# Scale and bias on VectorE in the last pair of heads, with four smaller moves of work in a fused attention, MoE and ELU kernel

## The chip, the core and the metric

The kernel runs on one core of one Trainium2 chip. The core has TensorE (matrix products, with a row of its own in the profile for the loading of weights), VectorE, ScalarE, GpSimd and SyncE, which work in parallel, each in the order of its own instruction list, and wait for each other through semaphores. The metric is the device time of one execution in microseconds (us), the median of several runs.

## What is computed

Three stages follow each other. In the reference, cut to what matters:

```python
# attention: 2 batches x 8 heads, 768 tokens, 64 channels; 6 random projections give each token a bucket
q_bucket = sum((q @ proj > 0) * 2**bit);  k_bucket = sum((k @ proj > 0) * 2**bit)
scores = where(q_bucket == k_bucket, q @ k.T / 8, -1e9)
attn = softmax(scores);  x = attn @ v                     # x: 1536 tokens x 512
# mixture of 8 experts, one for each token
e = argmax(x @ w_gate);  gate = softmax(x @ w_gate)[e];  eom = sigmoid(x @ w_output_gate)[e]
x = gate * eom * (relu(x @ w1[e]) @ w2[e])
# dense layer
h = x @ w_in;  out = where(h > 0, h, exp(min(h, 0)) - 1) @ w_out
```

## The kernel before

Attention goes through 96 query tiles of 128 tokens (8 pairs of heads, 12 tiles a pair), numbered n = 0 to 95. A hand-written software pipeline issues, in pass n of one loop, stages of several tiles; every engine then works off its own list in that order. For one tile the stages are:

- stage_S, TensorE: four matmuls give the 128 x 768 scores in PSUM (tile `s`, two buffers).
- stage_M: VectorE takes the negated row maximum `nm` of the scores (L369); GpSimd turns it into a scale `sc` (L370, zero or 2^64) and a bias `bi` (L371), one number for each of the 128 rows.
- stage_E, ScalarE: the exponential `p` of the scores with that bias and scale, and the row sums (L378).
- stage_T: six TensorE transposes of `p` into PSUM tiles `t` (three buffers, shared with some other small tiles); ScalarE copies each rounded to `pthi` (L402), VectorE makes the remainder `ptlo` (L405 for the second half of a tile, run one pass later, and L407 for the first half). A buffer `t` is free when `ptlo` is made.
- stage_V, TensorE: four matmuls a pass with the values `vst`; after three passes the output `o` is copied out (stage_O), in the last two pairs with an addition on VectorE (L447).

So in a pass VectorE does, in this order: `nm` of the tile before, the late `ptlo`, whatever was queued for this pass in the list `early`, the first `ptlo`. Other work is attached to passes by `at(n, f)`, which runs f at the end of pass n. The heads of the next pair are prepared on the way: `load_pair` loads them on SyncE's queue, `prep_T` splits them into `qhi`/`qlo` and `khi`/`klo` (one buffer each), and `restack` copies these by DMA into the operands `qa`, `qb`, `ka`, `kb`.

The gate of a batch (`gate`) is a list of small steps on 128 x 48 or 128 x 24 elements: logits, maximum, one-hot `oh`, softmax weight, rank of each token in its expert by matmuls into PSUM (`rank`), that rank times `oh` (`g_rk`), the row `rown`, its integer `idx`, and counts of tokens (`count`, `lt`, `count_lt`, `count_all`). The first batch's gate is spread over the passes 63 to 87 by `gate_first`; a scatter by row numbers `idx` follows from pass 85 on GpSimd. The second batch's gate runs in two halves after the last tile (gates 2 and 3). Expert 0's inputs from these halves are then gathered by matmuls with selection matrices `sel`: `part_rows` makes `row0` from `g_rk` and `oh` (L917), `part_sel` compares `row0` with `ranks` (L927), `part_rest` makes the remainders `xlo` (L937), and TensorE adds up `xacc` (L944). After that come the experts' products (from about 255 us) and the dense layer (to the end).

Of the kernel before, what the change touches and what calls it, by code (L numbers as in the profile page):

```python
# [13 lines left out]
ALU = mybir.AluOpType  # L14
AX = mybir.AxisListType
# [4 lines left out]
UNIT = float(2.0 ** 64)  # L20
# [5 lines left out]
def kernel(  # L26
# [19 lines left out]
    nc = tc.nc  # L46
# [14 lines left out]
    CAP = 224  # L61
# [6 lines left out]
    XC = DM + 16  # L68
# [7 lines left out]
    w8 = const.tile([128, E], F32, name="w8")  # L76
    nc.gpsimd.iota(w8, pattern=[[-1, E]], base=E, channel_multiplier=0, allow_small_or_imprecise_dtypes=True)
    ranks = const.tile([128, CAP], BF16, name="ranks")
    nc.gpsimd.iota(ranks, pattern=[[1, CAP]], base=0, channel_multiplier=0, allow_small_or_imprecise_dtypes=True)
    tok = const.tile([128, B, NC], I32, name="tok")  # L80
    nc.gpsimd.iota(tok, pattern=[[S, B], [1, NC]], base=0, channel_multiplier=NC)
    ones_b = const.tile([128, 128], BF16, name="ones_b")
# [3 lines left out]
    with nc.allow_low_precision("multiples of 256 below 2 ** 14 of at most 6 bits, exact"):  # L86
# [3 lines left out]
        tri_b, ones_b, pattern=[[1, 128]], compare_op=ALU.is_gt, fill=0.0, base=0, channel_multiplier=-1  # L90
# [60 lines left out]
    zt0 = ap1.tile([128, XC], F32, name="zt0")  # L151
# [210 lines left out]
    def stage_M(n):  # L362
        hd, c = tile_of(n)
        if c == 0:
            sums[hd] = ap2.tile([128, NC], F32, tag="sums", name="sums", bufs=3)
        nm = ap2.tile([128, 1], F32, tag="nm", name="nm", bufs=3)
        bi = ap2.tile([128, 1], F32, tag="bi", name="bi", bufs=3)
        sc = ap2.tile([128, 1], F32, tag="sc", name="sc", bufs=3)
        nc.vector.tensor_reduce(nm, sps[n][:, :, 0:HC], AX.XY, ALU.max, negate=True)  # L369
        nc.gpsimd.tensor_scalar(sc, nm, 0.25, UNIT, ALU.is_lt, ALU.mult)  # L370
        nc.gpsimd.tensor_tensor(bi, sc, nm, ALU.mult)  # L371
        soft[n] = (bi, sc)

    def stage_E(n):
# [161 lines left out]
    box = {}  # L536
# [3 lines left out]
    def gate(gi, n=HALF):  # L540
# [18 lines left out]
        eq, d, ed, oz, rk = (t3(x) for x in ("eq", "d", "ed", "oz", "rk"))  # L559
        lt = t3("lt", BF16)  # L560
        oh = ohs[:, gis].rearrange("p g c e -> p (g c) e")
        rw_n = rown[:, gis].rearrange("p g c -> p (g c)")
# [5 lines left out]
        V = nc.vector  # L568
        P = V if b == B - 1 else nc.gpsimd

        def rank():
            if n == HALF:
                ps = small_psum(sh, gi == NG - 2)
            else:
                ps = sps[max(sps)][:, 0, HC:HC + n * E].rearrange("p (c e) -> p c e", e=E)
            nc.tensor.matmul(ps, ones_b, eb_b[:, 0:n], start=True, stop=False)
            nc.tensor.matmul(ps, tri_b, oh, start=False, stop=False)
            for i in range(1, n):
                nc.tensor.matmul(ps[:, i:], ones_b, oh[:, :n - i], start=False, stop=(gi == 0 and i == n - 1))
            if gi:  # L580
                for i in range(n):
                    nc.tensor.matmul(ps[:, i], ones_b, cnt[:, gi, 0], start=False, stop=(i == n - 1))

            def mine():
                V.tensor_tensor(rk, ps, oh, ALU.mult)

            if n == HALF:
                mine()
            else:
                early.append(mine)  # L590

# [15 lines left out]
        def count_all():  # L607
# [16 lines left out]
            rank,  # L624
            weight,
            lambda: V.reciprocal(xg[:, :, DM:DM + 1], gg[:, :, None]),
            lambda: V.tensor_reduce(rw_n, rk, AX.X, ALU.add),
            lambda: V.tensor_copy(idx, rw_n),
        ]
        after = [  # L630
            count,
            lambda: V.tensor_tensor(lt, bc(fm), w8b, ALU.is_gt),
            count_lt,
            count_all,
        ]
# [7 lines left out]
            scat.append(i)  # L643
            spacer()

        box[gi] = (oh, rk, eq)
        return main, after, [lambda c=c: scatter(c) for c in range(n)]

    def spacer():
# [10 lines left out]
    def both(fs):  # L660
        for f in fs:
            f()

    load_pair(1, "q")
    def keep_warm(n, end=False):
        ps = (ps_t if end else ps_o).tile([128, HC], F32, tag="t" if end else "o", name="warm")
        for i in range(n):
# [25 lines left out]
    qhi_evac, qlo_evac = prep_T(0, "q", 1)  # L693
    qhi_evac()
    bit_weights()
    load_pair(0, "v")

    def place(nm, p0, t):
        nc.sync.dma_start(opnd[0, nm][p0:p0 + 64, HC:].bitcast(F32), t[0:64, HC:].bitcast(F32))
# [4 lines left out]
    def second_half():  # L704
        qlo_evac()
        place("qa", 64, qlo)
        for nm in "qk":
            prep_Zm(0, 1, nm)
        restack(0, "q", (1,))
        load_pair(1, "k")  # L710
        load_pair(1, "v")
# [10 lines left out]
    NQ = NH * NC  # L722
# [5 lines left out]
    def at(n, f, *a):  # L728
        todo.setdefault(n, []).append((f, a))
# [3 lines left out]
    def gate_first():  # L733
        main, after, scs = gate(0, NC)
        for n, fs in (
            (63, main[:4]), (64, main[5:6]), (67, main[4:5]), (73, main[6:10]), (75, main[10:11] + main[12:13] + after[:3]),
            (78, main[15:]), (79, main[11:12]), (81, main[13:14]), (82, main[14:15]), (87, after[3:]),
        ):
            for f in fs:
                at(n, f)  # L740
        for n, f in zip((85, 87, 88, 90, 91, 93), scs):
            at(n, f)
# [24 lines left out]
    for hh in range(2):  # L767
        at(10 + 2 * hh, joining_rows, rw, hh)
        at(14 + 4 * hh, joining_rows, rw_end, hh)
    for j in range(3):  # L770
        at(13 + 3 * j, nc.gpsimd.memset, zt0[:, j * XC // 3:(j + 1) * XC // 3], 0.0)
    for hh in range(2):
        at(12 + 3 * hh, load_gates, hh, False)
        at(61 + 3 * hh, load_gates, hh, True)
# [138 lines left out]
    parts = {}  # L913

    def part_rows(gi):
        oh, rk, _ = box[gi]
        nc.vector.scalar_tensor_tensor(parts[gi][0], rk[:, :, 0], -1.0, oh[:, :, 0], ALU.add, ALU.add)  # L917

    def part_tiles(gi):
        row0 = gate_p.tile([128, HALF], F32, tag="row0", name="row0", bufs=2)  # L920
# [582 lines left out]
```

## Time and profile before

| | |
|---|---|
| median of 3 runs | 704.16 us (703.58 to 704.34) |
| profiled execution, its own time | 704.39 us |
| its span, first to last instruction | 702.3 us |
| attention tiles (first to last `nm`) | 10.1 to 234.6 us |
| last pair (`nm` of tile 84 to `nm` of tile 95) | 209.25 to 234.56 us |
| granted TensorE clock, mean | 0.997 of full speed |

The profile covers one execution. Times in its rows are counted from the first instruction; 2.1 us of the execution's time lie outside the span. An entry in square brackets is the idle time of the engine before the instruction and what ended it.

### The profile page before, as it was taken

How to read it: one execution, taken by the hardware profiler on the slowest of the kernel's cores; microseconds unless marked ns; L12 is line 12 of the kernel's file. 1: busy time of each engine (PE TensorE's matmuls, PEld its weight loads, DVE VectorE, ACT ScalarE, POOL GpSimd, SP SyncE). 2: the span in 40 equal slices, each digit the busy share in tenths (PEclk: the TensorE clock that was granted, in tenths of full speed). 3: DMA queues.
4: the chain of work that ended last, by engine and by line, in shares of the span. 5: the costliest groups of instructions: out<-in, count | busy, mean ns of one | idle time of the engine just before them, and what ended most of it. 6: DMA issues, size and time to landing. Idle time of an engine off the chain costs nothing.

```text
span 702.3 us, 12093 instructions
## 1 busy us (share of the span) xinstructions
PE 688.6 (98%) x4120; PEld 616.4 (88%) x4121; DVE 553.1 (79%) x1026; ACT 427.8 (61%) x854; POOL 214.6 (31%) x503
## 2 busy tenths in 40 slices
PE   8999999999999999999999999999999999999996
PEld 5799999999999989999999998888888888888885
DVE  6999999999999897888888898877788447934433
ACT  5998998999888767666766664444543224422221
POOL 5676556555566640221235410000000000002012
PEclk9999999999999999999999999999999999999998
DMA  8747658667572259777788984222122000001011
GB/s 194 195 115 210 173 161 203 181 174 203 148 201 79 77 184 327 237 244 251 229 211 229 264 218 113 93 88 91 61 90 91 0 1 0 1 1 60 7 53 64
DMA packets 47476, 96.92 MB, mean 138 GB/s; under 512 B 11752, under 2 KB 23848, under 8 KB 47408
## 3 DMA queue, kind: packets, MB, share of 16 engines
q1 hardware_dynamic: 44944, 89.67, 45.2%
q0 software_dynamic: 2304, 6.40, 2.4%
q8 instruction: 35, 0.57, 0.3%
q14 instruction: 33, 0.27, 0.1%
q10 hardware_dynamic: 160, 0.00, 0.0%
HBM read 63.68 MB, written 10.72 MB: 106 GB/s over the span
## 4 chain that ended last, share of the span: by engine, by line
PE 52%; issue 34%; DMA 6%; DVE 5%; ACT 2%; POOL 1%; SPq 0%; DVEq 0%; POOLq 0%; ACTq 0%
PE hps L1186 12%; PE s L351 8%; PE yps L1199 8%; PE o L421 8%; PE t L400 7%; DMA out_dram<-part,tidt 5%; PE yps L1201 3%; PE sp L501 2%; DVE nm L369 2%; PE zps L280 1%; PE xTp L1168 1%; DVE ptlo L407 1%; DMA qb<-qhi 1%; DMA tidt<-tid_d 1%; PE xacc L944 1%
## 5 line engine op out<-in xcount | busy, mean ns | idle before, releaser
L378 ACT ACTIVATE p<-s,bi,sc 128x768 f32<-128x768 f32 x96 | 95.8, 998 | 4.7 <-POOL bi L371 4.3
L886 DVE TENSOR_TENSOR wl<-wraw,wh 128x1024 fp32r<-128x1024 f32 (+1 forms) x65 | 77.2, 1190 | 21.8 <-ACT wh L882 19.6
L1344 POOL DMA_INDIRECT out_dram<-part,tidt x12 | 11.5, 959 | 265.4 <-DVE part L1341 264.2
L369 DVE TENSOR_REDUCE nm<-s 128x1 f32<-128x768 f32 x96 | 90.6, 944 | 2.0 <-POOL vst L330 1.1
L1306 ACT ACTIVATE ee<-gps 128x512 f32<-128x512 f32 x48 | 28.7, 597 | 100.1 <-PE gps L1296 100.1
L402 ACT ACTIVATE pthi<-t 128x384 fp32r<-128x384 f32 x192 | 84.0, 493 | 7.6 <-PE t L400 6.3
L1199 PE MATMUL yps<-h,wh 128*128 128x448 f32 x256 | 84.5, 380 | 0.0
L400 PE MATMUL t<-ident,p 128*128 128x128 f32 x576 | 80.3, 273 | 2.0 <-DVE ptlo L405 1.1
L1296 PE MATMUL gps<-x2l,vh 128*128 128x512 f32 x192 | 75.9, 395 | 0.0
L1326 PE MATMUL a<-vh,gl 128*128 128x512 f32 x192 | 75.8, 395 | 0.0
L1296 PE MATMUL gps<-x2h,vl 128*128 128x512 f32 x192 | 75.7, 394 | 0.0
L1296 PE MATMUL gps<-x2h,vh 128*128 128x512 f32 x192 | 75.7, 394 | 0.0
L1326 PE MATMUL a<-vh,gh 128*128 128x512 f32 x192 | 75.5, 393 | 0.0
L1326 PE MATMUL a<-vl,gh 128*128 128x512 f32 x192 | 75.5, 393 | 0.0
L351 PE MATMUL s<-ka,qa 128*128 128x384 f32 x192 | 73.3, 383 | 1.8 <-DMA qa<-qlo 1.2
L400 PEld LDWEIGHTS t<-ident,p 128*128 128x128 f32 x576 | 68.1, 140 | 7.8 <-PE t L400 1.5
L1307 DVE TENSOR_SCALAR ee<-ee 128x512 f32<-128x512 f32 x48 | 20.4, 426 | 68.0 <-ACT ee L1306 67.9
L1309 ACT ACTIVATE gh<-ee 128x512 fp32r<-128x512 f32 x48 | 30.4, 633 | 69.0 <-DVE ee L1308 69.0
L421 PE MATMUL o<-pthi,vst 128*128 128x384 f32 x192 | 66.9, 348 | 0.3
L882 ACT ACTIVATE wh<-wraw 128x1024 fp32r<-128x1024 f32 x63 | 66.2, 1052 | 0.0
L351 PE MATMUL s<-kb,qb 82*128 82x384 f32 x192 | 65.2, 340 | 0.0
L421 PE MATMUL o<-ptlo,vst 128*128 128x384 f32 x192 | 64.9, 338 | 0.0
(238 smaller groups left out, 1783.9 us busy)
## 6 DMA issues: line engine op xcount, KB each, us to landing
wraw<-in_moe_w_t_dram SPq DMA_DIRECT2D x64, 512.0 KB
w<-in_moe_w_in_dram SPq DMA_DIRECT2D x16, 512.0 KB
w<-in_moe_w_out_dram SPq DMA_DIRECT2D x16, 512.0 KB
ka<-khi SPq DMA_DIRECT2D x30, 192.0 KB
xs_d<-zt SPq DMA_DIRECT2D x8, 528.0 KB
xs<-xs_d SPq DMA_DIRECT2D x7, 462.0 KB
raw_v<-in_v_dram SPq DMA_DIRECT2D x8, 384.0 KB
kb<-klo SPq DMA_DIRECT2D x15, 192.0 KB
```

The lines of the kernel that those rows point to most:

```text
L351: nc.tensor.matmul(ps[:, j, 0:HC], opnd[st, "q" + x][0:n1, cb], opnd[st, "k" + x][0:n1, j * HC:(j + 1) * HC], start=(x == "a"), stop=(x == ...
L369: nc.vector.tensor_reduce(nm, sps[n][:, :, 0:HC], AX.XY, ALU.max, negate=True)
L378: nc.scalar.activation(p.rearrange("p (a b) -> p a b", a=2), sps.pop(n)[:, :, 0:HC], AF.Exp, bias=bi, scale=sc, accum_out=sums[hd][:, c:c ...
L400: nc.tensor.transpose(ps[:, a, :], p[:, kt * 128:(kt + 1) * 128], ident)
L402: nc.scalar.activation(ho, ps, AF.Copy)
L421: nc.tensor.matmul(ops[m], vst[hd][:, kt, :], t[:, kt, :], start=(kt == 0 and x == 0), stop=(kt == NC - 1 and x == 1))
L882: eng_hi.activation(hi, r, AF.Copy)
L886: fs = [lambda c=slice(j, j + h): eng.tensor_tensor(lo[:, c], r[:, c], hi[:, c], ALU.subtract) for j in range(0, PW, h)]
L1186: nc.tensor.matmul(ps, w[:, dc, fs], x[:, dc], start=(i == 0), stop=(i == len(terms) - 1))
L1199: nc.tensor.matmul(ps, wh[:, f], h[:, :, f], start=(f == 0), stop=last)
L1296: nc.tensor.matmul(ps, w[:, dc], x[:, dc, th * TC:(th + 1) * TC], start=(dc == 0 and i == 0), stop=(dc == KD - 1 and i == 2),)
L1326: nc.tensor.matmul(ps, x[:, cs], w, start=(fb in first_fb and i == 0), stop=(fb in last_fb and i == 2))
```

## The change

Five edits:

1. In the last pair (passes that handle tiles 84 to 95) `sc` and `bi` are made on VectorE instead of GpSimd.
2. In the first batch's gate the counts `count`, `lt` and `count_lt` move from pass 75 to passes 86 and 87, `count_all` from 87 to 90, and `rown` and `idx` from pass 78 to 82.
3. For gates 2 and 3 `row0` is made straight from the rank sums in PSUM, `(ps + 1) * oh`, with `ranks` counted from 1 instead of 0; the product `g_rk` moves behind it, in front of `rown`.
4. On SyncE's queue the values of pair 0 are loaded where the transposed queries of pair 1 were, and those queries behind the copy of `qlo`.
5. The zero tile `zt0` is cleared in six pieces of 88 columns instead of three of 176.

```diff
-    nc.gpsimd.iota(ranks, pattern=[[1, CAP]], base=0, ...)
+    nc.gpsimd.iota(ranks, pattern=[[1, CAP]], base=1, ...)
...
         nc.vector.tensor_reduce(nm, sps[n][:, :, 0:HC], AX.XY, ALU.max, negate=True)
-        nc.gpsimd.tensor_scalar(sc, nm, 0.25, UNIT, ALU.is_lt, ALU.mult)
-        nc.gpsimd.tensor_tensor(bi, sc, nm, ALU.mult)
+        eng = nc.vector if n >= NQ - 12 else nc.gpsimd
+        eng.tensor_scalar(sc, nm, 0.25, UNIT, ALU.is_lt, ALU.mult)
+        eng.tensor_tensor(bi, sc, nm, ALU.mult)
...
             if n == HALF:
-                mine()
+                box[gi] = (oh, ps)
+                late.append(mine)
...
-            lambda: V.tensor_reduce(rw_n, rk, AX.X, ALU.add),
+            lambda: (both(late), V.tensor_reduce(rw_n, rk, AX.X, ALU.add)),
...
-    load_pair(1, "q")
+    load_pair(0, "v")
...
     bit_weights()
-    load_pair(0, "v")
...
         place("qa", 64, qlo)
+        load_pair(1, "q")
...
-            (63, main[:4]), (64, main[5:6]), (67, main[4:5]), (73, main[6:10]), (75, main[10:11] + main[12:13] + after[:3]),
-            (78, main[15:]), (79, main[11:12]), (81, main[13:14]), (82, main[14:15]), (87, after[3:]),
+            (63, main[:4]), (64, main[5:6]), (67, main[4:5]), (73, main[6:10]), (75, main[10:11] + main[12:13]),
+            (79, main[11:12]), (81, main[13:14]), (82, main[14:]), (86, after[:1]), (87, after[1:3]), (90, after[3:]),
...
-    for j in range(3):
-        at(13 + 3 * j, nc.gpsimd.memset, zt0[:, j * XC // 3:(j + 1) * XC // 3], 0.0)
+    for j in range(6):
+        at(11 + 3 * j // 2, nc.gpsimd.memset, zt0[:, j * XC // 6:(j + 1) * XC // 6], 0.0)
...
-        nc.vector.scalar_tensor_tensor(parts[gi][0], rk[:, :, 0], -1.0, oh[:, :, 0], ALU.add, ALU.add)
+        nc.vector.scalar_tensor_tensor(parts[gi][0], ps[:, :, 0], 1.0, oh[:, :, 0], ALU.add, ALU.mult)
```

Lines of the changed kernel stand one to four further down than those of the kernel before (`ptlo` L405 and L407 are L406 and L408 there). On SyncE's queue, the first loads of the program, before:

```order
L135 DMA raw_q<-in_q_dram 128x3x64 x4
L130 DMA raw_q<-in_q_t_dram 128x768
L303 DMA ka_134<-khi 64x768 x2
L303 DMA kb_135<-klo 64x768
L126 DMA raw_v<-in_v_dram 128x2x384
L699 DMA qa_128<-qhi 64x384
L699 DMA qb_129<-qhi 64x384
L699 DMA qa_128<-qlo 64x384
L303 DMA qa_132<-qhi 64x768
L303 DMA qa_132<-qlo 64x768
L303 DMA qb_133<-qhi 64x768
```

The same place with the change:

```order
L135 DMA raw_q<-in_q_dram 128x3x64 x4
L126 DMA raw_v<-in_v_dram 128x2x384
L303 DMA ka_134<-khi 64x768 x2
L303 DMA kb_135<-klo 64x768
L701 DMA qa_128<-qhi 64x384
L701 DMA qb_129<-qhi 64x384
L701 DMA qa_128<-qlo 64x384
L130 DMA raw_q<-in_q_t_dram 128x768
L303 DMA qa_132<-qhi 64x768
L303 DMA qa_132<-qlo 64x768
L303 DMA qb_133<-qhi 64x768
```

The values have moved three transfers forward, and pair 1's queries (`in_q_t_dram`) six, to just ahead of the three copies that restack head 1 of pair 0.

On VectorE, the passes around tile 86 (where `nm` of a tile, the two `ptlo`, the reciprocal of a row sum and the addition of an output follow each other), before:

```order
L369 TENSOR_REDUCE nm<-s 128x1
L405 TENSOR_TENSOR ptlo<-t,pthi 128x3x128
L407 TENSOR_TENSOR ptlo<-t,pthi 128x3x128
L468 RECIPROCAL ri<-sm 128x3
L369 TENSOR_REDUCE nm<-s 128x1
L405 TENSOR_TENSOR ptlo<-t,pthi 128x3x128
L447 TENSOR_TENSOR osb<-o,osb 64x384
L407 TENSOR_TENSOR ptlo<-t,pthi 128x3x128
```

The same place with the change:

```order
L369 TENSOR_REDUCE nm<-s 128x1
L371 TENSOR_SCALAR sc<-nm 128x1
L372 TENSOR_TENSOR bi<-sc,nm 128x1
L406 TENSOR_TENSOR ptlo<-t,pthi 128x3x128
L408 TENSOR_TENSOR ptlo<-t,pthi 128x3x128
L469 RECIPROCAL ri<-sm 128x3
L605 TENSOR_REDUCE cnt<-ohs 128x8
L369 TENSOR_REDUCE nm<-s 128x1
L371 TENSOR_SCALAR sc<-nm 128x1
L372 TENSOR_TENSOR bi<-sc,nm 128x1
L406 TENSOR_TENSOR ptlo<-t,pthi 128x3x128
L448 TENSOR_TENSOR osb<-o,osb 64x384
```

Behind each of the last twelve `nm` stand two more instructions, the second of which reads the result of the first, and `cnt` (pass 86) is now here; `g_lt` and the second `cnt` follow one pass later.

On VectorE after the last tile, gate 3's end (`g_gg` is the weight, `xlo` a remainder for the gather), before:

```order
L594 SCALAR_TENSOR_TENSOR g_gg<-g_ez,g_se 128x3
L626 RECIPROCAL xlast<-g_gg 128x3
L585 TENSOR_TENSOR g_rk<-sp,ohs 128x24
L917 SCALAR_TENSOR_TENSOR row_4230<-g_rk,ohs 128x3
L927 TENSOR_SCALAR sel<-ranks,row_4230 128x224
L937 SCALAR_TENSOR_TENSOR xlo<-xw,xhi 128x512
L927 TENSOR_SCALAR sel<-ranks,row_4230 128x224
L937 SCALAR_TENSOR_TENSOR xlo<-xw,xhi 128x512
L627 TENSOR_REDUCE rown<-g_rk 128x3
```

The same place with the change:

```order
L598 SCALAR_TENSOR_TENSOR g_gg<-g_ez,g_se 128x3
L630 RECIPROCAL xlast<-g_gg 128x3
L920 SCALAR_TENSOR_TENSOR row_4233<-sp,ohs 128x3
L930 TENSOR_SCALAR sel<-ranks,row_4233 128x224
L940 SCALAR_TENSOR_TENSOR xlo<-xw,xhi 128x512
L930 TENSOR_SCALAR sel<-ranks,row_4233 128x224
L940 SCALAR_TENSOR_TENSOR xlo<-xw,xhi 128x512
L588 TENSOR_TENSOR g_rk<-sp,ohs 128x24
L631 TENSOR_REDUCE rown<-g_rk 128x3
```

`g_rk` has left the place in front of `row0` and stands between the last `xlo` of gate 2 and `rown`.

## Rows read from the trace of the kernel before

**Rows 1.** The page, part 1: busy time, share of the span, instructions.

```profile
PE 688.6 (98%) x4120; PEld 616.4 (88%) x4121; DVE 553.1 (79%) x1026; ACT 427.8 (61%) x854; POOL 214.6 (31%) x503
```

**Rows 2.** Last pair: length; busy PE, PEld, DVE, ACT, POOL; clock, DMA share, GB/s.

```profile
209.20:236.20 27.00, 26.50 (x177) 25.01 (x176) 25.26 (x47) 23.52 (x52) 17.46 (x47) 1.00 0.24 86
```

**Rows 3.** Waits of TensorE's weight loads, 215 to 240: total, times, longest.

```profile
PEld o L421 <- DVE osb L447: 0.9, 2, 0.5
```

**Rows 4.** Waits of ScalarE, 209.2 to 236.2: total, times, longest.

```profile
ACT p L378 <- POOL bi L371: 0.3, 1, 0.3
```

**Rows 5.** Timeline of TensorE at the end of the last pair: start, duration, instruction.

```profile
236.10 1.54 PE L501 MATMUL sp<-rw_end,osb 128*128 128x80 f32 x12 [0.25 <-DVE ptlo L405]
```

**Rows 6.** Timeline of VectorE, one pass of the pair before.

```profile
196.66 0.95 DVE L369 TENSOR_REDUCE nm<-s 128x1 f32<-128x768 f32 x1
197.53 0.55 DVE L405 TENSOR_TENSOR ptlo<-t,pthi 128x384 fp32r<-128x384 f32 x1
197.99 0.55 DVE L407 TENSOR_TENSOR ptlo<-t,pthi 128x384 fp32r<-128x384 f32 x1
198.45 0.17 DVE L468 RECIPROCAL ri<-sm 128x3 f32<-128x3 f32 x1
```

**Rows 7.** Timeline of VectorE, last pair: tile 84, an evacuation, the last pass.

```profile
209.25 0.95 DVE L369 TENSOR_REDUCE nm<-s 128x1 f32<-128x768 f32 x1
...
226.15 0.55 DVE L528 TENSOR_TENSOR xw<-sp,ri 128x384 f32<-128x384 f32 x1
...
236.14 1.02 DVE L407 TENSOR_TENSOR ptlo<-t,pthi 128x384 fp32r<-128x384 f32 x2 [0.18 <-ACT pthi L402]
```

**Rows 8.** Groups of VectorE, 209.2 to 236.7: busy, mean ns, idle before.

```profile
L407 DVE TENSOR_TENSOR ptlo<-t,pthi 128x384 fp32r<-128x384 f32 x14 | 7.7, 557 | 1.7 <-ACT pthi L402 1.4
...
L447 DVE TENSOR_TENSOR osb<-o,osb 64x384 f32<-64x384 f32 x2 | 1.1, 560 | 0.4 <-ACT osb L446 0.3
```

**Rows 9.** Timeline of VectorE in gate 2: small instructions behind each other.

```profile
238.95 0.18 DVE L612 TENSOR_REDUCE g_mx<-lg 128x3 f32<-128x24 f32 x1
239.17 0.18 DVE L613 TENSOR_TENSOR g_eq<-lg,g_mx 128x24 f32<-128x24 f32 x1
...
243.56 0.18 DVE L626 RECIPROCAL xw<-g_gg 128x3 f32<-128x3 f32 x1
243.66 0.18 DVE L585 TENSOR_TENSOR g_rk<-sp,ohs 128x24 f32<-128x24 f32 x1
```

**Rows 10.** Timeline of VectorE, the first batch's gate, passes 76 and 79.

```profile
186.69 0.23 DVE L601 TENSOR_REDUCE cnt<-ohs 128x8 bf16<-128x48 bf16 x1
...
187.26 0.96 DVE L369 TENSOR_REDUCE nm<-s 128x1 f32<-128x768 f32 x1
...
194.09 0.19 DVE L627 TENSOR_REDUCE rown<-g_rk 128x6 f32<-128x48 f32 x1
...
194.40 0.95 DVE L369 TENSOR_REDUCE nm<-s 128x1 f32<-128x768 f32 x1
```

**Rows 11.** Timeline of TensorE's weight loads behind these steps.

```profile
190.71 0.31 PEld L400 LDWEIGHTS t<-ident,p 128*128 128x128 f32 x3 [0.57 <-PE t L400]
```

**Rows 12.** Timeline of SyncE's queue at the start: issue time and its length.

```profile
5.04 0.48 SPq L130 DMA_DIRECT2D raw_q<-in_q_t_dram  x1
...
8.27 1.11 SPq L126 DMA_DIRECT2D raw_v<-in_v_dram  x1
...
13.33 0.60 SPq L303 DMA_DIRECT2D qb<-qhi  x1
```

**Rows 13.** Timeline of all engines at the start: two waits for transfers.

```profile
15.85 0.41 PE L351 MATMUL s<-ka,qa 128*128 128x384 f32 x1 [1.25 <-DMA qa<-qlo]
...
17.87 0.52 ACT L218 ACTIVATE qhi<-raw_q 128x384 fp32r<-128x384 f32 x1 [1.24 <-DMA qb<-qhi]
```

**Rows 14.** Timelines of VectorE and of TensorE's weight loads in gate 3.

```profile
248.50 0.15 DVE L585 TENSOR_TENSOR g_rk<-sp,ohs 128x24 f32<-128x24 f32 x1
...
251.18 2.07 DVE L937 SCALAR_TENSOR_TENSOR xlo<-xlast,xhi 128x512 fp32r<-128x512 f32 x3
...
253.31 0.74 PEld L944 LDWEIGHTS xacc<-sel,xlo 128*128 128x128 f32 x6 [0.20 <-DVE xlo L937]
```

More of the change, by code (lines that the diff above doesn't have):

```diff
@@ L78 @@
     ranks = const.tile([128, CAP], BF16, name="ranks")
-    nc.gpsimd.iota(ranks, pattern=[[1, CAP]], base=0, channel_multiplier=0, allow_small_or_imprecise_dtypes=True)
+    nc.gpsimd.iota(ranks, pattern=[[1, CAP]], base=1, channel_multiplier=0, allow_small_or_imprecise_dtypes=True)
     tok = const.tile([128, B, NC], I32, name="tok")
@@ L569, in gate @@
         P = V if b == B - 1 else nc.gpsimd
+        late = []
         def rank():
@@ L644, in scatter @@
             spacer()
-        box[gi] = (oh, rk, eq)
         return main, after, [lambda c=c: scatter(c) for c in range(n)]
@@ L915, in part_rows @@
     def part_rows(gi):
-        oh, rk, _ = box[gi]
-        nc.vector.scalar_tensor_tensor(parts[gi][0], rk[:, :, 0], -1.0, oh[:, :, 0], ALU.add, ALU.add)
+        oh, ps = box[gi]
+        nc.vector.scalar_tensor_tensor(parts[gi][0], ps[:, :, 0], 1.0, oh[:, :, 0], ALU.add, ALU.mult)
     def part_tiles(gi):
```

## The prediction, made before the changed kernel was run

> **What bounds the kernel now.** The busy shares come first [rows 1]: TensorE is at 98% of the span, so over most of it nothing that spares another engine can show. The change lies in attention, which ends at about 237 us, and in the 18 us behind it, so I read those stretch by stretch. The busy times of the last pair [rows 2] show TensorE at 26.50 of 27.00 us, VectorE at 25.26, ScalarE at 23.52 and GpSimd at 17.46: two engines are close to full, GpSimd is not. Then I ask who waited there. TensorE lost 0.9 us to VectorE's output addition [rows 3]; ScalarE lost 0.3 us to GpSimd's `bi`, once in twelve tiles [rows 4]. So GpSimd's hand-over, which the first edit shortens, holds back almost nothing, and VectorE already does. At the end of the pair TensorE stands waiting for VectorE's `ptlo` [rows 5]: what VectorE loses in these passes, TensorE loses too. At the start of the program two waits are for transfers [rows 13].
>
> **Scale and bias on VectorE.** Its price on VectorE: in a full pass `nm`, late `ptlo` and first `ptlo` take 0.87, 0.46 and 0.46 us from start to start, 1.79 together [rows 6]; an instruction that needs nothing of `nm` starts 0.08 us before `nm` ends. `sc` does need it. In the gate [rows 9] an instruction that reads the one in front (`g_eq` behind `g_mx`) starts 0.22 us after a start of 0.18 us duration, so 0.04 us after its end; one that does not read it (`g_rk` behind the reciprocal) starts after 0.10 us. So `sc` starts 0.95 + 0.04 = 0.99 us after `nm`, 0.12 more than now; `bi` 0.17 + 0.04 = 0.21 us later, with the duration of the small reciprocal of [rows 6]; the late `ptlo` about 0.09 behind `bi`. That is 0.4 us a tile, 4.8 us for twelve. The counts, moved into the same passes, took 187.26 - 186.69 = 0.57 us [rows 10]. Together 5.4 us more for VectorE.
>
> What can take it up is VectorE's idle time. From tile 84's `nm` at 209.25 to the end of the first of the two `ptlo` at 236.14, 236.65, are 27.4 us [rows 7]. The needed steps are 12 x 1.79 = 21.5, four reciprocals at 0.1, two output additions at 0.56 [rows 8], two evacuations at 0.55 [rows 7] with a smaller one of about 0.2 each: 24.5 us. So 2.9 us are free. The visible idle time is less, 27.00 - 25.26 = 1.74 [rows 2], since a busy instruction's tail hides short gaps. I take 2.9, because start-to-start steps are what the engine needs: 5.4 - 2.9 = **+2.5 us**, between +1.9 (free time 3.3, without the smaller evacuations, and 0.2 us off the added work) and +3.7 (only 1.74 free). It reaches TensorE in full, because TensorE's last pass already waits for VectorE [rows 5]. Queued behind `sc` and `bi` are the two `ptlo`, for whose buffers the next transposes wait. The earlier bias is worth at most the 0.3 us of [rows 4] and is buried under this.
>
> The Trainium skill, "VectorE: DVE Perf Modes", section "The TRN2 errata", prices an SBUF instruction of VectorE at 58 cycles plus the elements at 0.96 GHz, an estimate of 61 ns for one element, 1.5 us for the 24. By it the added 1.5 + 0.57 us would fit into the free 2.9 and the last pair would lose nothing. The trace does not agree: its small instructions last 0.17 to 0.18 us [rows 6, 9].
>
> **The first batch's gate.** Behind the counts VectorE works through two passes without an idle time in its rows, and TensorE stood 0.57 us at 190.71 for a transpose buffer that VectorE had still to read [rows 11]. Without the counts that read is 0.57 us earlier; `rown` and `idx`, 194.40 - 194.09 = 0.31 us [rows 10], leave the same full stretch for pass 82, where VectorE has idle time. TensorE gets back at most 0.57 + 0.31 = 0.9 and at least 0.3; I take **-0.7 us**, most of the sum, since VectorE is full there. GpSimd's count in pass 90 has no reader before gate 2.
>
> **Start.** TensorE's fourth tile waits 1.25 us for `qa<-qlo`, and 2 us later ScalarE waits 1.24 us for the restack `qb<-qhi`, which still reads the one buffer `qhi` [rows 13]. The edit takes pair 1's queries out of the queue in front of `qa<-qlo`, so the first wait shrinks. But it puts them in front of the restack: the same bytes lie ahead of `qb<-qhi` as before, and its issue, at 13.33 us, comes a query issue of 0.48 us later [rows 12]. Between kb's copy and the first `qhi` copy the queue now has nothing to issue where the values stood (8.27 us, [rows 12]), and 384 KB move out of that gap to behind 12 us. ScalarE's list is in order: pair 1's `qhi` stands ahead of tile 1's `pthi`, so all that follows waits for the later of the two transfers. Bounds: 0 if the DMA engines never run dry, 0.8 us if they idle for most of the moved transfer. I take the issue, **+0.5 us**. The values themselves were waited for by nobody.
>
> **Row numbers.** `g_rk` leaves the path to `sel`: 0.19 us earlier. But VectorE is full from there to the last three `xlo` at 251.18 [rows 14], `g_rk` only moves in front of `rown`, which reads it, and TensorE's last wait is for those `xlo` [rows 14]: 0.0, within 0.1 either way. The smaller clears of `zt0` are off every path I found: 0.
>
> **Sum.** 2.5 - 0.7 + 0.5 = +2.3 us on the profiled execution's 704.39, that is 706.7. That execution stands 0.23 us above the median of the runs, 704.16, so the forecast for the median is 706.5 us.
>
> **Rivals.**
> - *The last pair takes it up (not slower).* If `sc` and `bi` cost VectorE only the unread step of 0.10 us each [rows 9], they add 12 x 0.2 + 0.57 = 3.0 us, as much as is free. The point of decision is (2.9 - 0.57) / 12 = 0.19 us a tile. Then the pair gives 0 to -0.9 [rows 3], the whole -0.2 to -1.1: 703.1 to 704.0 us. For it: the two are tiny and no row shows a 128 x 1 operation on VectorE. Against: every row of a reader behind its writer shows the wait. By the formula of the Trainium skill's "VectorE: DVE Perf Modes", section "The TRN2 errata", this case would come true.
> - *Every wait goes (faster).* The restack lands no later, the fourth tile's 1.2 us count in full, the gate gives 0.7 and the last pair the 0.9 of [rows 3]: -2.8, 701.4 us. Against: ScalarE's wait at 17.87 comes after the fourth tile's, and the transfer it waits for is issued later.
> - *Dearer.* Only the visible idle time takes up work (+3.7), the restack is 0.8 late, the gate gives 0.3: +4.2, 708.4 us.
> - *The hand-over is no sooner.* The first `ptlo` waits 1.4 us for ScalarE in the pair [rows 8]. If VectorE, though later, still meets these waits, the free time that they hold cannot be used, and `sc` and `bi` hand over no sooner than GpSimd did: 2.9 - 1.4 = 1.5 us are taken up, the pair costs 3.9 us, the whole 3.7: 707.9 us. Against: an engine that comes later finds its input ready.
>
> **Numbers.** 0.50 for the forecast with its own range 705.2 to 707.7, 0.21 for the taken-up case, 0.13 for faster, 0.10 for dearer, 0.06 for the hand-over no sooner. The range takes in the taken-up case with half a microsecond below it and goes up nearly to the dearer case: 702.6 to 708.2 us leaves out most of the faster case and half of the dearer, 0.16 or so. This kernel's measurement cannot tell 0.2% (1.4 us) from no change. Above 705.6 lie the dearer case, the late hand-over and most of the forecast's (0.39): slower 0.55. Within 702.8 to 705.6 lie the forecast's rest (0.11) and most of the taken-up case (0.15): 0.26. Faster: 0.13 and the low edge of the taken-up case, 0.06, together 0.19.
>
> **What the profile will show.** If I am right, the last twelve `nm` are 0.4 us further from the late `ptlo` (about 1.27 instead of 0.87), VectorE is busy without a visible gap from tile 84 to the pair's end, TensorE's waits for `ptlo` in the pair grow to some 2 us, and `nm` 84 to `nm` 95 takes 27.5 instead of 25.3 us. The wait of 0.57 us at pass 76 is gone. At the start the fourth tile's wait is under 0.5 us and pair 1's first `qhi` starts at about 18.4 instead of 17.87. The last `xlo` is made as long after gate 3's start as now. I am wrong if `sc` and `bi` stand under 0.2 us a tile, if TensorE ran so far ahead that the pair ends on time, or if `qhi` starts before 17.8.

## The result, and the profile after

The changed kernel takes **711.17 us** (median of 5 runs, 710.25 to 711.95); the kernel before, on the same chip, 703.58 us (703.50 to 704.34). The ratio is 1.0104, 95% interval 1.009 to 1.0117: the change makes the kernel slower by 7.6 us. The forecast was slower by 2.3 us, in a range that ended at 708.2.

The profiled execution of the changed kernel took 711.17 us with a span of 709.1, against 704.39 and 702.3 before. Where the 6.8 us went is read from the start times of the same instructions in the two traces (after minus before, and below for the experiments too):

| kernel | `nm` of tile 4 | tile 75 | tile 80 | tile 84 | tile 95 | first product `hps` of the experts | last scatter |
|---|---|---|---|---|---|---|---|
| changed kernel | +1.48 | +1.72 | +1.43 | +1.52 | +5.49 | +6.26 | +6.78 |
| e1: scale and bias | -0.57 | -0.67 | -0.67 | -0.67 | +2.77 | +3.57 | +3.55 |
| e2: order of loads | +1.40 | +1.56 | +1.56 | +1.58 | +1.61 | +1.61 | +1.83 |
| e3: gate | -0.30 | -0.29 | -0.57 | -0.46 | -0.05 | -0.06 | -0.08 |
| e4: row numbers, clears | -0.61 | -0.57 | -0.58 | -0.57 | -0.57 | -0.61 | -0.61 |
| e5: bias by pointer | -0.57 | -0.62 | -0.63 | -0.62 | +2.23 | +2.68 | +2.58 |
| e6: values late | -0.33 | +2.17 | +2.15 | +2.16 | +2.16 | +2.14 | +2.06 |
| e7: swapped loads | -0.33 | -0.43 | -0.44 | -0.43 | -0.39 | -0.40 | -0.39 |
| e8: loads and fillers | +1.66 | +1.56 | +1.56 | +1.57 | +1.58 | +1.54 | +1.44 |
| e9: all but the loads | -0.42 | -0.54 | -0.82 | -0.72 | +3.23 | +4.00 | +3.98 |
| e10: scale, bias and gate | -0.96 | -0.97 | -1.25 | -1.16 | +2.83 | +3.61 | +3.60 |
| e11: e1, a cast on ScalarE | -0.31 | -0.37 | -0.39 | -0.38 | +2.18 | +2.97 | +3.06 |

Kernels that load as before (e1, e3, e4, e5, e9, e10, e11) stand at -0.3 to -1.0 in tile 4: the profiled execution of before was late at the start, so a column is read against its row's tile 4, not against zero. This lateness is that of the two waits of [rows 13]. None of the seven traces shows the first, for `qa<-qlo`, and in the second ScalarE waits 0.20 to 0.41 us there instead of 1.24. Timeline of ScalarE, e9:

```profile
17.44 0.53 ACT L218 ACTIVATE qhi<-raw_q 128x384 fp32r<-128x384 f32 x1 [0.24 <-DMA qb<-qhi]
```

So in the changed kernel the start costs 1.7 us against that one execution, but 2.3 us against e9, which differs in the loads alone (tile 75: +1.72 and -0.54). The gate takes 0.2 back by tile 84, the last pair with its hand-over costs 6.26 - 1.52 = 4.74, gates 2 and 3 nothing more (the last `lp` of attention and `hps` both stand at +6.26), and 0.5 comes in the experts' phase. Together 2.3 - 0.2 + 4.7 + 0.5 = 7.3 of the 7.6 us between the medians.

Page of the changed kernel, part 1 (answers [rows 1]):

```profile
PE 689.8 (97%) x4120; PEld 616.8 (87%) x4121; DVE 557.8 (79%) x1050; ACT 428.8 (60%) x854; POOL 208.1 (29%) x482
```

The 24 new instructions raise VectorE's busy time by 4.7 us; TensorE's is nearly unchanged, so the time lost is waiting.

**The start.** Timeline of SyncE's queue, changed kernel (answers [rows 12]):

```profile
7.25 0.54 SPq L303 DMA_DIRECT2D kb<-klo  x1
9.81 0.46 SPq L701 DMA_DIRECT2D qa<-qhi  x1
...
12.18 0.58 SPq L130 DMA_DIRECT2D raw_q<-in_q_t_dram  x1
...
13.96 0.60 SPq L303 DMA_DIRECT2D qb<-qhi  x1
```

Between kb's copy and the first `qhi` copy nothing is issued. Windows of half a microsecond, changed kernel; the last three columns are TensorE's granted clock, DMA share and GB/s:

```profile
10.00:10.50 0.50, 0.50 (x5) 0.50 (x4) 0.28 (x1) 0.00 (x0) 0.41 (x2) 1.00 0.27 80
...
12.00:12.50 0.50, 0.50 (x4) 0.50 (x3) 0.50 (x1) 0.50 (x1) 0.50 (x2) 1.00 0.07 19
```

The same windows of the kernel before:

```profile
10.00:10.50 0.50, 0.50 (x5) 0.50 (x4) 0.41 (x1) 0.00 (x0) 0.41 (x2) 1.00 0.98 203
...
12.00:12.50 0.50, 0.50 (x5) 0.39 (x3) 0.38 (x1) 0.50 (x1) 0.50 (x2) 1.00 0.92 332
```

The windows behind each of the two read 0.11 and 0.38 now and 0.98 and 0.86 before. In these four half microseconds the DMA engines were nearly full before and are mostly idle now. From 10 to 13 us their mean share is 0.38, against 0.89 before and 0.84 in e9: an estimate from these shares is that 1.4 to 1.5 us of the three were lost to transfers. That is most of the restack's delay: the `qhi` that waits for it starts 1.48 us later than before, and 1.91 later than in e9. Timeline of all engines, changed kernel (answers [rows 13]):

```profile
19.35 0.52 ACT L218 ACTIVATE qhi<-raw_q 128x384 fp32r<-128x384 f32 x1 [2.58 <-DMA qb<-qhi]
...
20.99 0.75 PE L401 MATMUL t<-ident,p 128*128 128x128 f32 x3 [2.86 <-DVE ptlo L408]
```

The fourth tile's wait for `qa<-qlo` is gone, and `nm` of tile 3 is 1.06 us earlier than before; but that wait is absent from the kernels that load as before too, whose tile 3 is 0.4 to 1.2 us earlier, so this is not the edit's gain. ScalarE's wait has grown to 2.58 us, from 1.24 before and 0.24 in e9, and TensorE stands idle for 2.86 us behind it. Windows of the changed kernel behind this idle time:

```profile
21.00:22.00 1.00, 1.00 (x4) 0.68 (x5) 1.00 (x2) 1.00 (x4) 0.12 (x1) 0.60 0.00 0
22.00:23.00 1.00, 1.00 (x4) 1.00 (x4) 1.00 (x3) 0.97 (x4) 0.92 (x3) 0.50 0.00 0
...
25.00:26.00 1.00, 1.00 (x8) 0.97 (x7) 1.00 (x3) 0.80 (x2) 0.94 (x3) 1.00 1.03 197
```

Behind the idle time the granted clock fell to 0.50, the lower level of 1.2 GHz, and was back at 2.4 GHz at 25 us.

**The last pair.** Windows, changed kernel (answers [rows 2]), then waits in it: total, times, longest (answers [rows 3 to 5]):

```profile
210.70:241.80 31.10, 27.16 (x176) 24.58 (x174) 29.80 (x73) 24.18 (x52) 13.24 (x23) 1.00 0.21 74
```

```profile
PE o L422 <- DVE osb L448: 2.4, 2, 1.3
PE sp L502 <- DVE ptlo L406: 0.9, 1, 0.9
ACT p L379 <- DVE bi L372: 0.7, 2, 0.5
```

VectorE is busy for 29.80 of 31.10 us, and of the 1.3 us left some 0.8 are the gaps in front of `sc` and `bi` (24 of 0.03). TensorE waits 2.4 us for VectorE's additions and 0.9 us for its remainders, and once more just behind this window:

```profile
242.40 0.87 PE L502 MATMUL sp<-rw_end,osb 128*128 128x80 f32 x6 [1.02 <-DVE ptlo L406]
```

That makes 4.3 us, most of the pair's 4.74. The 0.9 + 1.0 for `ptlo` are the 2 us that were forecast; the 2.4 for `osb` were not. `nm` 84 to `nm` 95 takes 29.3 us, not 27.5.

Timeline of VectorE and GpSimd in the changed kernel (answers [rows 6, 7]), an ordinary pass, one of the moved counts (`g_lt`, with `cnt` behind it up to the next `nm`), and the three places where `bi` is long:

```profile
213.53 1.02 POOL L432 TENSOR_TENSOR osb<-o,o 64x384 f32<-64x384 f32 x1
214.12 0.45 DVE L372 TENSOR_TENSOR bi<-sc,nm 128x1 f32<-128x1 f32 x1
...
218.53 0.20 DVE L636 TENSOR_TENSOR g_lt<-g_fm,w 128x48 bf16<-128x48 f32 x1
...
218.92 0.95 DVE L369 TENSOR_REDUCE nm<-s 128x1 f32<-128x768 f32 x1
...
221.10 0.94 DVE L369 TENSOR_REDUCE nm<-s 128x1 f32<-128x768 f32 x1
222.08 0.15 DVE L371 TENSOR_SCALAR sc<-nm 128x1 f32<-128x1 f32 x1
222.27 0.16 DVE L372 TENSOR_TENSOR bi<-sc,nm 128x1 f32<-128x1 f32 x1
222.35 0.55 DVE L406 TENSOR_TENSOR ptlo<-t,pthi 128x384 fp32r<-128x384 f32 x1
...
234.94 1.04 POOL L887 CAST wh<-wraw 128x1024 fp32r<-128x1024 f32 x1
234.98 1.01 DVE L372 TENSOR_TENSOR bi<-sc,nm 128x1 f32<-128x1 f32 x1
...
239.24 2.53 POOL L889 TENSOR_TENSOR wl<-wraw,wh 128x512 fp32r<-128x512 f32 x2
...
241.23 0.55 DVE L372 TENSOR_TENSOR bi<-sc,nm 128x1 f32<-128x1 f32 x1
```

An ordinary tile goes from `nm` to the late `ptlo` in 0.98 + 0.19 + 0.08 = 1.25 us instead of 0.87, as forecast. But `bi`, one number a row, takes 0.45, 1.01 and 0.55 us in three of the twelve tiles, and each of the three ends when a GpSimd instruction ends: 214.57 against 214.55, 235.99 against 235.98, 241.78 against 241.77. `sc`, which has one input, stands beside the same addition of 213.53 and takes 0.16 us.

The trace of before has a hold like this already, with the engines exchanged. Timelines of GpSimd and VectorE, before:

```profile
20.73 0.57 POOL L371 TENSOR_TENSOR bi<-sc,nm 128x1 f32<-128x1 f32 x1
20.70 0.55 DVE L222 SCALAR_TENSOR_TENSOR qlo<-raw_q,qhi 128x384 fp32r<-128x384 f32 x1
```

GpSimd's `bi` took 0.19 us in 69 of the 96 tiles and 0.39 to 0.58 us in 27. Each of the 27 started behind VectorE's `qlo` or `klo`, which read two tensors in SBUF, and ended 0.05 us after it. The rows picked for the prediction show none of these.

**The gate.** Timeline of VectorE and of TensorE's matmuls and weight loads, changed kernel (answers [rows 10, 11]):

```profile
188.67 0.27 PE L582 MATMUL s<-ohs,ones_b 128*128 128x40 bf16 x5
188.98 0.96 DVE L369 TENSOR_REDUCE nm<-s 128x1 f32<-128x768 f32 x1 [0.48 <-PE s L582]
...
192.42 0.31 PEld L401 LDWEIGHTS t<-ident,p 128*128 128x128 f32 x3 [0.57 <-PE t L401]
...
205.63 0.16 DVE L631 TENSOR_REDUCE rown<-g_rk 128x6 f32<-128x48 f32 x1
...
205.91 0.95 DVE L369 TENSOR_REDUCE nm<-s 128x1 f32<-128x768 f32 x1
```

Where the counts stood VectorE now waits 0.48 us for TensorE: not for the scores, whose last matmul starts at 187.73, but for the rank matmuls of this gate (L582). They write into spare columns of the tile `s` that `nm` reads, and end at 188.94. Before, the counts filled this wait. TensorE's wait of 0.57 us is there as before. Only `rown` and `idx` gave something, 0.3 us from tile 78 on, and took it back in front of tile 82.

**Gates 2 and 3.** Timeline of VectorE and of TensorE's weight loads, changed kernel (answers [rows 14]):

```profile
254.67 0.18 DVE L630 RECIPROCAL xlast<-g_gg 128x3 f32<-128x3 f32 x1
...
257.44 2.07 DVE L940 SCALAR_TENSOR_TENSOR xlo<-xlast,xhi 128x512 fp32r<-128x512 f32 x3
...
259.56 0.74 PEld L947 LDWEIGHTS xacc<-sel,xlo 128*128 128x128 f32 x6 [0.36 <-DVE xlo L940]
```

The last `xlo` start 257.44 - 254.67 = 2.77 us behind the reciprocal of the weights, exactly as before, where that reciprocal starts at 248.41 (251.18 - 248.41).

### The profile page after: what moved, and what is told of

Its sections match the earlier page's. It is cut to its first block, busy times and chain, and to the rows that moved or that the text cites. A ratio compares the mean times of both kernels' runs of the same rounds, so it can differ in the third digit from the quotient of the medians.

```text
span 709.1 us, 12080 instructions
## 1 busy us (share of the span) xinstructions
PE 689.8 (97%) x4120; PEld 616.8 (87%) x4121; DVE 557.8 (79%) x1050; ACT 428.8 (60%) x854; POOL 208.1 (29%) x482
## 4 chain that ended last, share of the span: by engine, by line
PE 49%; issue 34%; DVE 8%; DMA 6%; ACT 1%; POOL 1%; SPq 1%; DVEq 0%; ACTq 0%; POOLq 0%
PE hps L1189 11%; PE s L351 8%; PE yps L1202 8%; PE o L422 7%; PE t L401 7%; DMA out_dram<-part,tidt 5%; PE yps L1204 3%; DVE nm L369 2%; PE sp L502 2%; PE zps L280 1%; DVE ptlo L406 1%; DVE ptlo L408 1%; PE xTp L1171 1%; DMA qb<-qhi 1%; DMA tidt<-tid_d 1%
```

## The experiments

Each kernel is the kernel before with the edit shown. Times are medians of 5 to 11 runs, against 9 to 21 runs of the kernel before on the same chip. Costs of a stage are read from the table above.

### e1: scale and bias alone

```diff
+        eng = nc.vector if n >= NQ - 12 else nc.gpsimd
-        nc.gpsimd.tensor_scalar(sc, ...); nc.gpsimd.tensor_tensor(bi, sc, nm, ALU.mult)
+        eng.tensor_scalar(sc, ...); eng.tensor_tensor(bi, sc, nm, ALU.mult)
```

> The kernel before with only the scale and the bias of the last twelve tiles on VectorE. Theory A (the edits cost what they cost each by itself; this one fills VectorE, and the bias with its two SBUF inputs now and then stands while GpSimd works): 4.0 to 4.8 us slower, nm of tile 84 to nm of tile 95 about 29 us instead of 25.3, one to three bias instructions of 0.4 us or more instead of 0.16. Theory B (the edits only hurt together: without the counts in the pair and without the shifted start there is room): 1 to 2.5 us slower. Rival from the forecast (the pair takes it up): 0 to 1 us faster.

Measured: 708.06 against 703.94 us, ratio 1.0059 (1.0046 to 1.0073), +4.1 us; the pair costs 3.57 + 0.67 = 4.24 us. The same three `bi` are long (0.46, 1.01 and 0.55 us). So this edit makes more than half of the loss, without the counts.

### e2: order of the first loads alone

```diff
-    load_pair(1, "q")
+    load_pair(0, "v")
...
     bit_weights()
-    load_pair(0, "v")
...
         place("qa", 64, qlo)
+        load_pair(1, "q")
```

> The kernel before with only the order of the first loads changed. Theory A (the queue has nothing to move between the copy of klo and that of qlo, so the DMA engines idle, and the restack that pair 1's qhi waits for lands later by the time of the moved transfer): 1.6 to 1.8 us slower, ScalarE's first qhi of pair 1 at about 19.35 instead of 17.87, TensorE at half clock for some 3 us behind it. Theory B (only the later issue counts, as forecast): 0.5 us slower. Rival: the fourth tile's wait counts: 1 us faster.

Measured: 706.28 against 703.94 us, ratio 1.0042 (1.0028 to 1.0056), +2.3 us, by the medians more than theory A's 1.6 to 1.8. In the trace tile 6 comes 2.2 us later than in e1, which loads as before (25.54 against 23.39 us); nothing of that is given back, and 0.2 us more go in the experts' phase. The wait is the changed kernel's:

```profile
19.28 0.52 ACT L218 ACTIVATE qhi<-raw_q 128x384 fp32r<-128x384 f32 x1 [2.46 <-DMA qb<-qhi]
```

### e3: the gate's moved steps alone

```diff
-  (75, main[10:11] + main[12:13] + after[:3]), (78, main[15:]), ... (82, main[14:15]), (87, after[3:]),
+  (75, main[10:11] + main[12:13]), ... (82, main[14:]), (86, after[:1]), (87, after[1:3]), (90, after[3:]),
```

> The kernel before with only the steps of the first batch's gate moved. Theory A (the full stretch at passes 75 to 79 gets 0.3 us back at first, pass 82 takes it again, and the counts at 86 and 87 use idle time of VectorE while GpSimd still makes scale and bias): within 0.4 us of before. Theory B (as forecast, the gain stays): 0.5 to 0.9 us faster. Theory C (the counts in the pair hurt by themselves): 0.3 to 0.6 us slower.

Measured: 704.12 against 703.94 us, ratio 1.0004 (0.9995 to 1.0013): no change. Against its own start (-0.30) it gains 0.3 from tile 78, loses that at tile 82, finds some 0.15 by tile 83 and loses 0.4 in the last pair, where the counts now stand. So they found no idle time there, though theory A's total came out.

### e4: row numbers and smaller clears alone

```diff
-        nc.vector.scalar_tensor_tensor(parts[gi][0], rk[:, :, 0], -1.0, oh[:, :, 0], ALU.add, ALU.add)
+        nc.vector.scalar_tensor_tensor(parts[gi][0], ps[:, :, 0], 1.0, oh[:, :, 0], ALU.add, ALU.mult)
```

with the rest of edits 3 and 5.

> The kernel before with only the row numbers from the rank sums and the zero tile in six pieces. Theory A (VectorE is full there and the product only changes its place): within 0.2 us of before. Rival (TensorE's selection matmuls start sooner and end sooner): 0.2 to 0.4 us faster.

Measured: 703.95 against 703.94 us, ratio 1.0000 (0.9991 to 1.0009), and the same distance to before from the first tiles to the end.

### e5: the bias with a pointer scalar

```diff
-        eng.tensor_tensor(bi, sc, nm, ALU.mult)
+        eng.tensor_scalar(bi, nm, sc, None, ALU.mult)
```

On top of e1, for these twelve tiles. The product is the same; `sc` is read as one number for each row, not as a second tensor.

> As e1_scale_bias, but the bias is made with one SBUF tensor and a pointer scalar, bi = nm * sc[row], instead of two SBUF tensors. Theory A (a bias with two SBUF tensors cannot start while GpSimd works, and stood 0.3, 0.85 and 0.4 us so): all twelve bias instructions last 0.16 to 0.2 us, and the kernel is 0.8 to 1.5 us faster than e1_scale_bias, 2.6 to 3.3 us slower than before. Theory B (the three long ones have another cause, such as a late semaphore): the same three are long, 4.1 us slower than before.

Measured: 707.09 against 703.82 us, ratio 1.0047 (1.0033 to 1.006), +3.3 us; the pair costs 2.68 + 0.62 = 3.30 instead of 4.24 us. Timeline of GpSimd and VectorE at the place of e1's longest `bi`:

```profile
232.38 1.04 POOL L888 CAST wh<-wraw 128x1024 fp32r<-128x1024 f32 x1
232.47 0.21 DVE L373 TENSOR_SCALAR bi<-nm,sc 128x1 f32<-128x1 f32 x1
232.60 0.55 DVE L409 TENSOR_TENSOR ptlo<-t,pthi 128x384 fp32r<-128x384 f32 x1
```

All twelve take 0.21 us, also beside the same cast. The hold belongs to the form with two tensor inputs from SBUF. The form costs 0.05 us more in every tile (0.13 instead of 0.08 to `ptlo`), so 1.5 us of holds go and 0.6 come: 0.9 us, as measured.

### e6: the values of pair 0 late

```diff
     bit_weights()
-    load_pair(0, "v")
...
         restack(0, "q", (1,))
+        load_pair(0, "v")
         load_pair(1, "k")
```

> The kernel before with pair 0's values loaded behind the restack of pair 0's head 1; pair 1's queries stay early. Theory A (the start hangs on the restack that reads qhi, and on the bytes and idle time of the queue ahead of it): ScalarE's wait for it (1.24 us) shrinks to under 0.5 us, 0.7 to 1.2 us faster. Rival (GpSimd then waits for the values at tile 3 and holds up the scale and bias queued behind them): 0.5 us slower to 0.3 us faster.

Measured: 706.09 against 703.82 us, ratio 1.0034 (1.0021 to 1.0046): slower by 2.3 us. The rival named the cause, but the size lies outside both forecasts. Timeline of GpSimd and TensorE, e6:

```profile
19.37 0.29 POOL L329 CAST vst<-raw_v 128x128 fp32r<-128x128 f32 x1 [3.23 <-DMA raw_v<-in_v_dram]
...
21.83 0.44 PE L351 MATMUL s<-ka,qa 128*128 128x384 f32 x1 [2.11 <-ACT p L378]
```

Theory A had nothing to win: ScalarE waits 0.27 us for the restack, as it does in the kernels that load as before. The values' rounding stands ahead of a tile's `sc` on GpSimd's list: that `sc` starts at 20.16 us, against 18.00 before and 17.22 in e1, and the exponential behind it is late. The values are on the path after all if they come this late. One thing more: the queue has an empty gap here too (DMA share 0.55 over 10 to 13 us), and `qhi` starts on time, at 17.53 us. So a gap alone does not delay the restack; in e2 a transfer stands between the two as well.

### e7: values and queries change places

```diff
-    load_pair(1, "q")
+    load_pair(0, "v")
...
     bit_weights()
-    load_pair(0, "v")
+    load_pair(1, "q")
```

As many bytes stand ahead of each copy as before, and the queue has something to issue where the values stood.

> The kernel before with pair 0's values and pair 1's queries in each other's place in the queue: the values as early as in the changed kernel, but the same bytes ahead of every copy of qlo and qhi as before and no dry queue. Theory A (the loss of e2_load_order comes from the queue that runs dry and the moved bytes ahead of the restack): within 0.4 us of before. Theory B (early values are bad in themselves, since they move the first copies of khi): 1 us slower or more.

Measured: 703.85 against 703.82 us, ratio 1.0001 (0.9992 to 1.001). Timeline of SyncE's queue and ScalarE:

```profile
8.59 0.81 SPq L130 DMA_DIRECT2D raw_q<-in_q_t_dram  x1
...
17.54 0.53 ACT L218 ACTIVATE qhi<-raw_q 128x384 fp32r<-128x384 f32 x1 [0.27 <-DMA qb<-qhi]
```

Early values alone cost nothing; the wait is the 0.2 to 0.4 us of the kernels that load as before. What costs is the place of pair 1's queries, behind 12 us with an empty gap before them.

### e8: the changed order of loads with a busy TensorE

e2, and at the end of pass 4 fourteen matmuls of ones that nobody reads:

```diff
+    at(4, keep_warm, 14)
```

> As e2_load_order, with 14 filler matmuls on TensorE behind the scores of tile 4, where it waits 2.7 us and then runs at half clock to about 25 us. Theory A (the slow clock adds 0.2 us to the 1.4 us of the late transfer): the granted clock stays at 1.0, 0.1 to 0.3 us faster than e2_load_order. Rival (the slow clock makes most of the loss): 1 us faster than e2_load_order or more. Third way (the filler itself is late): slower than e2_load_order.

Measured: 706.00 against 703.82 us, ratio 1.0031 (1.002 to 1.0043), +2.2 us. Windows:

```profile
22.00:23.00 1.00, 1.00 (x7) 0.86 (x7) 1.00 (x3) 0.97 (x4) 0.85 (x3) 1.00 0.00 0
```

With TensorE busy in front, the clock stays at 2.4 GHz, and the loss is 2.2 instead of 2.3 us, a difference inside the noise. In the traces e2 loses 0.17 us more than e8 between `qhi` (19.28 and 19.53) and tile 6, and 0.25 by tile 75. So the half clock is worth some 0.2 us, and the late transfer the rest.

### e9 and e10: the large terms together

e9 is the changed kernel with the loads ordered as before; e10 is e1 with e3.

> All edits but the order of the first loads (scale and bias on VectorE, the gate's moved steps, row numbers from rank sums, smaller clears). Theory A, the two large terms add up: the order of the loads is worth here what it is worth alone, +2.3 us, so this kernel stands at about +5.3 (709.0 us); row maximum of tile 84 at -0.6 to -0.9 against before, of tile 95 at +3.7 to +4.1, so the last pair costs 4.7 as in the changed kernel, since a longer last pair does not depend on when it starts. Rival B: in the changed kernel the late start and the last pair lie over each other or add to each other (other phases of VectorE against GpSimd): then the pair costs 4.2 or less, and this kernel stands at +4.3 or below. Separate question, the 0.5 us that the changed kernel loses between the first product of the experts and the end: if it belongs to the edits kept here it shows again (end later by 0.4 to 0.6 than the first product is); if it is a chance of one execution or belongs to the loads, it is under 0.2.

> Scale and bias on VectorE in the last pair and the gate's moved steps, nothing else. Theory A, the counts come on top of scale and bias where VectorE is already full: the pair costs 4.7 us instead of 4.2, and the gate's 0.3 is given back before it, so +4.5 to +4.8 (708.5 us). Rival B, the counts find a gap in the pair and the gate's gain stays: pair 4.2, +3.6 to +4.0 (707.7 us).

Measured: e9 708.48 against 703.76 us, ratio 1.0069 (1.0056 to 1.0083), +4.7 us, between the two forecasts; e10 708.05, ratio 1.0061 (1.0047 to 1.0074), +4.3, between them too. The pair itself answers for theory A in both: 4.00 + 0.72 = 4.72 and 3.61 + 1.16 = 4.77 us, against 4.24 in e1 without the counts. The order of the loads is then worth 7.6 - 4.7 = 2.9 us in the changed kernel, 0.6 more than alone. The traces split this into 2.3 at the start (tile 75) and the 0.5 of the experts' phase, which e9 does not show (3.98 at its end, 4.00 at its start).

### e11: the cast beside tile 93's bias on ScalarE

```diff
-    at(NQ - 2, lambda: split_piece(0, nc.gpsimd, nc.gpsimd, rest0))
+    at(NQ - 2, lambda: split_piece(0, nc.gpsimd, nc.scalar, rest0))
```

On top of e1.

> Scale and bias on VectorE in the last pair (as e1), and the rounding of an expert's weight piece that GpSimd does beside the bias of tile 93 (128x1024, 1.04 us) made on ScalarE instead; nothing else on VectorE or GpSimd changes. Theory A, the bias with two tensors from SBUF waits for the GpSimd instruction that runs beside it: the long bias of tile 93 (1.01 us in e1) falls to 0.16, while the two beside GpSimd's other work (tiles 85 and 95, 0.46 and 0.55 us in e1) stay at 0.4 to 0.6; the pair costs 3.4 to 3.8 us instead of 4.24, less than 0.85 back if ScalarE's 1.05 us more hold up an exponential; 707.2 to 707.7 us. Rival B, the bias of tile 93 is long for a reason of its own place (a buffer, a wait that the profile does not show): it stays at about 1.0 us and the pair at 4.2 or more; 708.0 us or above.

Measured: 707.44 against 703.89 us, ratio 1.0051 (1.0037 to 1.0064), +3.5 us; the pair costs 2.97 + 0.38 = 3.35 instead of 4.24 us, a little less than theory A said. Timeline of VectorE and GpSimd, `bi` of tiles 93 and 95:

```profile
234.70 0.16 DVE L372 TENSOR_TENSOR bi<-sc,nm 128x1 f32<-128x1 f32 x1
...
235.92 2.52 POOL L887 TENSOR_TENSOR wl<-wraw,wh 128x512 fp32r<-128x512 f32 x2
237.92 0.54 DVE L372 TENSOR_TENSOR bi<-sc,nm 128x1 f32<-128x1 f32 x1
```

Without GpSimd's cast beside it the bias of tile 93 takes 0.16 us, the other two are held as before (0.44 in tile 85), and the whole 0.85 us comes back. The hold is shown from both sides: by what runs on GpSimd here, by the form of the instruction in e5.

## Why the prediction was wrong, step by step

The direction was right, for the reason given: VectorE fills up in the last pair and TensorE waits for it. Three terms were mis-sized.

- **The pair, +2.5 forecast, +4.7 measured.** The steps of `sc` and `bi` are 0.38 us a tile against 0.40 (4.6 in all), the counts 0.13 + 0.39 = 0.52 against 0.57; both held, 0.3 us under the forecast. Missing was a cost of the operation: `bi` held behind GpSimd, 0.3 + 0.85 + 0.4 = 1.5 us. And the free time was 1.9 us, not 2.9: near the visible idle time of 1.74, which the working put aside. The 1.9 is no row, but what is left over (4.6 + 0.5 + 1.5 - 4.7); worked out so, e1, e5, e9, e10 and e11 give 1.8 to 1.9 as well, with holds and without. Of the missing 1.0 some 0.3 lies around the two additions `osb`, which start 0.58 us behind their neighbour and hold the next as long (0.46 and 0.56 were assumed), and 0.3 in two waits of `nm` for scores that remained; the rest has no row here. The sum 2.5 + 1.5 + 1.0 - 0.3 gives 4.7. The range's upper bound of +3.7 had the visible idle time, but not the hold.
- **The start, +0.5 forecast, +2.3 measured** (e2's median, and the changed kernel against e9). The path and the late instruction were named rightly; the size was taken from the issue, 0.5 us. The restack lands by what lies ahead in the queue and by when it was put there. `qhi` waited until 19.35, not 18.4: the DMA engines were mostly idle for 2 us, more than the bound of 0.8 allowed for. The two waits that the working started from were those of one execution; against the 17.44 us of e9 `qhi` is 1.9 us late.
- **The gate, -0.7 forecast, about 0 measured.** "VectorE works through two passes without an idle time" was wrong just ahead of those passes: the counts filled a wait of 0.48 us for the rank matmuls. Rows of a busy engine don't tell whether it would have waited without the work. The 0.31 of `rown` and `idx` was real and came back at tile 82, and the counts cost 0.5 in the pair, as charged there.
- **Row numbers, 0.0, and the clears, 0:** right, in e4 and in the rows of gate 3.

Of the rivals none came. For the pair that takes it up, 0.19 us a tile was the point of decision and 0.38 was measured; the rows show durations of 0.15 and 0.16 us and steps of 0.19. The estimate from the Trainium skill, "VectorE: DVE Perf Modes", section "The TRN2 errata", 61 ns for one element, would have made it true; but the same section says that this formula gives too little for a single instruction, with a measured fixed term of about 150 cycles, an estimate of 0.16 us, and the rows agree with that. "Every wait goes" counted a wait of 1.2 us that only the profiled execution of before has. The dearer case had the free time nearly right, but not the hold and not the size of the late restack. "The hand-over is no sooner" would have cost the pair 3.9; but of ScalarE's 0.7 us of waits for `bi` here 0.5 stand behind the longest hold, and without holds the pair costs less (e5, e11).

**What stays open.** The last 0.5 us, in the experts' phase. Timeline of the changed kernel there:

```profile
396.04 3.71 POOL L914 TENSOR_SCALAR xs<-xs 112x512 f32<-112x512 f32 x2 [10.57 <-DMA xs<-xs_d]
396.69 1.63 DVE L889 TENSOR_TENSOR wl<-wraw,wh 128x1024 fp32r<-128x1024 f32 x1
...
398.67 0.37 PE L1189 MATMUL hps<-xTh,wh 128*128 128x224 f32 x1 [0.37 <-DVE h L1192]
```

Timeline of the kernel before, the same instructions:

```profile
390.44 1.22 DVE L886 TENSOR_TENSOR wl<-wraw,wh 128x1024 fp32r<-128x1024 f32 x1
390.70 4.13 POOL L911 TENSOR_SCALAR xs<-xs 112x512 f32<-112x512 f32 x2 [11.48 <-DMA xs<-xs_d]
```

Before, VectorE's split started first and GpSimd took 4.13 us; now GpSimd starts first and takes 3.71, VectorE's two-input `wl` takes 1.63 instead of 1.22, and TensorE waits 0.37 us for the `h` behind it. The 0.4 has changed sides. That reads like the hold of the last pair, set off by when a transfer lands; it was not tested, and 0.15 us of the 0.5 have no row. A long `wl` alone does not cost: e1 has three of 1.42 to 1.65 us in this phase, and its TensorE stays at +3.57 throughout.

## What to carry to other kernels

Before an operation is moved to an engine near its limit, ask what its form does beside the other engines: a two-input operation on VectorE was held by GpSimd here, and one on GpSimd by VectorE, while the pointer-scalar form of the same product was not. Look for it in the kernel before: the same operation, on the other engine, may show it. A wait that one execution shows should be found in a second one before it is counted. Free time should be charged at the visible idle time until rows show more, and a gain from removed work needs the question of what the engine would have waited for in its place. A load moved later in a queue is charged by the bytes it takes out of a gap that then stands empty, not by the length of its issue.

## What the runs showed of the hardware

- A 128x1 product with two SBUF tensors on VectorE took 0.16 us, and 0.44 to 1.01 us beside three GpSimd instructions (an addition, a cast, a subtraction); with one tensor and a pointer scalar 0.21 us always (e1, e5, e11). A two-input `bi` beside GpSimd's indirect DMA (226.58 to 227.63 us in the changed kernel) took 0.16 us. On GpSimd the same product took 0.19 us, and 0.39 to 0.58 us in 27 tiles beside VectorE's `qlo` and `klo` (before). Not every meeting ends so: VectorE's two-input `wl` at 324.08 us started within a GpSimd `xs` (323.24 to 324.81 us) and took 1.22 us, as most do (before); what tells such places apart is not shown. The Trainium skill, "GPSIMD Engine Reference", section "1. Specifications", says that GpSimd's SBUF interfaces are shared with VectorE and that instructions with two SBUF inputs contend for them; the traces agree, and the longest hold here is the whole rest of a GpSimd instruction, 0.85 us.
- An instruction that reads the result of the one in front started 0.04 us after its end (`sc`, `bi`), one that does not 0.08 us before it: 0.12 us for the dependence.
- TensorE's idle time of 2.86 us was followed by some 3 us at 1.2 GHz; with the loads in the same order and 14 matmuls of no use in that time the clock stayed at 2.4 GHz (e8), and some 0.2 us were won, since TensorE still waited for others.
